# DeltaNet attention and a feed-forward block on one core: a fourth G buffer, key loads from GpSimd's queue, 16-token blocks for chunks 2 and 3, and a new start

## Chip, cores, metric

One core of one Trainium2 chip. The metric is the device time of one launch in microseconds (us). Engines: PE is TensorE, PEld its weight loads, DVE is VectorE, ACT is ScalarE, POOL is GpSimd, SP is SyncE (SPq its queue of transfers).

## The reference, cut to what matters

```python
# q, k, v: (4, 8, 768, 48) fp32; beta: (4, 8, 768)
k_n = k / (norm(k) + 1e-6)
for t in range(768):                      # per batch and head
    y[t]  = q[t] @ state
    v_old = k_n[t] @ state
    state = state + beta[t] * outer(k_n[t], v[t] - v_old)
x  = y as (4, 768, 384)                   # heads side by side
xn = (x - mean) / sqrt(var + 1e-6) * g_ln
out = x + relu(xn @ w_ch1) @ w_ch2        # 384 -> 1536 -> 384; the weights arrive as float64
```

## The kernel before

The 768 tokens are 12 chunks of 64. For a chunk, `p_g` is keys times keys and queries; the triangular matrix made of it is inverted in small diagonal blocks on DVE (lines `tmp` and `xb`), the blocks are put together with matmuls (`p_e`, `p_z`: the join) into `xt`, and then the recurrence runs (`p_by`, `p_u`, `p_s`), which needs the state of the chunk before. Every chunk is followed by its feed-forward (FFN) part, `p_h` and `p_o`, which is the bulk of PE's work. Chunks go in pairs: one inverse serves two. "Boundary" below means the place where a new pair's recurrence starts, seen as the first `p_u` of chunks 2, 4, 6, 8 and 10.

```python
def load_turned(c):                                   # 8 key and 8 query pieces per chunk
    load_blocks(k, c, 0, (nc.sync,))
    load_blocks(q, c, 1, (nc.sync,))
...
def new_chunk(c):
    gsb = work.tile([128, GH, C], FP32, name="gsb", bufs=3)
...
def prep(c):                                          # p_g of a chunk, and what leads to it
    new_chunk(c)
    for n in range(2):
        with tc.issue_after(after) if c < 4 else nullcontext():
            turned(c, n)                              # 32x32 transposes of keys, queries
        yield
    for g in range(2):
        products(c, g, 0, 2)                          # p_g
        yield
    ...
...
with in_this_order(tc) as last:                       # the start is traced in a fixed order
    ...
    joins = [first_join(c) for c in two]              # chunks 0 and 1 joined together
...
plan = Plan()                                         # all else: each step has a planned time
...
for m in range(1, NSL):                               # pairs of chunks
    times = (t - 102, t - 76, t - 38, t - 10) if m > 1 else (4, 22, 58, 74)
    if m > 1:
        for i, c in enumerate(chunks):
            plan.once(times[0] - 20 + 32.5 * i, load_turned, c)
    plan.spread(in_turn(*(prep(c) for c in chunks)), SLAB * N_PREP, times[0], times[1])
    plan.spread(blocks(m, (nc.sync,)), N_BLOCKS + 1, times[1], times[2])   # 32-token blocks
    plan.spread(join(chunks), 5, times[3], t)
plan.run()
```

The plan only fixes the order in which the program is traced. The builder then orders each engine's instructions by its own reckoning of when their inputs will be there; the traces show the engines at work in that built order (in the changed kernel all 848 DVE instructions of the page; of PE's records outside the joins, 6,181 of 6,184).

Of the kernel before, what the change touches and what calls it, by code (L numbers as in the profile page):

```python
# [8 lines left out]
FP32 = mybir.dt.float32  # L9
# [7 lines left out]
C = 64  # L17
DP = 64
BK = 32
FB = 16  # L20
SLAB = 2
# [46 lines left out]
def in_turn(*gens):  # L68
    for gen in gens:
        yield from gen  # L70
# [3 lines left out]
def kernel(  # L74
# [21 lines left out]
    nc = tc.nc  # L96
# [5 lines left out]
    KC = DM // 128  # L102
    FT = DFF // 128
    NP = H // 2
    GH = 2 * H
    TOK = 256

    const = ctx.enter_context(tc.tile_pool(name="const", bufs=1))
    loads = ctx.enter_context(tc.tile_pool(name="loads", bufs=3))
    work = ctx.enter_context(tc.tile_pool(name="work", bufs=2))  # L110
# [29 lines left out]
    def load_blocks(src, c, n, engs):  # L140
        dst = tblocks[(2 * c + n) % NTB]
        for u in range(2):
            toks = slice(c * C + 32 * u, c * C + 32 * u + 32)
            for hp in range(2):
                for m in range(2):
                    w = min(32, D - 32 * m)
                    p0 = DP * hp + 32 * m
                    engs[m % len(engs)].dma_start(  # L148
                        out=dst[p0 : p0 + 32, :, u, 0:w],
                        in_=src[:, hp::2, toks, 32 * m : 32 * m + w].rearrange("b j t d -> t (b j) d"),  # L150
                    )
# [11 lines left out]
    def load_kv(c):  # L163
        load(k_of(c), k, c)
        vs[c] = loads.tile([128, GH, D], FP32, name="v_raw")
        load(vs[c], v, c)

    def load_turned(c):
        load_blocks(k, c, 0, (nc.sync,))
        load_blocks(q, c, 1, (nc.sync,))  # L170

    for i in (0, 2, 1, 3):
        for hp in range(2):
            p0 = DP * hp + 32
# [17 lines left out]
    def fetch_words():  # L192
        if len(words) < len(pieces):
            words.append(early_pool.tile([128, WN, 2], U32, name="words", bufs=3))
            nc.gpsimd.dma_start(
                out=words[-1].rearrange("p n w -> p (n w)"), in_=pieces[len(words) - 1][1]
            )

    for _ in range(2):
        fetch_words()  # L200


    beta_b = const.tile([128, NSL, BK], FP32, name="beta_b")

    beta_f = const.tile([128, 2, FB], FP32, name="beta_f")

    def places():

# [2 lines left out]
                for i in range(2):  # L211
                    yield ((cc * 2 + e) * 2 + i) * GH, cc, e, i

    with nc.allow_non_contiguous_dma(reason="short rows of beta and g_ln"):
        for c in range(2):
            for e in range(2):
                nc.gpsimd.dma_start(
                    out=beta_f[e * C : (e + 1) * C, c],
                    in_=beta[2 * e : 2 * e + 2, :, c * C : (c + 1) * C]
                    .rearrange("g h (b t) -> b (g h) t", t=FB),  # L220
                )
        g_sb = const.tile([128, KC], FP32, name="g_sb")
        nc.gpsimd.dma_start(out=g_sb, in_=g_ln.rearrange("(t p) -> p t", p=128))

    def load_beta():
# [13 lines left out]
    for e in range(2):  # L239
        rows = slice(e * C, (e + 1) * C)  # L240
# [5 lines left out]
    xts = [const.tile([128, GH, C], FP32, name=f"xt{i}") for i in range(NXT)]  # L246
# [4 lines left out]
    states = [const.tile([128, 2, NP, D], FP32, name=f"s{g}") for g in range(2)]  # L251
    for t in states:
        nc.gpsimd.memset(t, 0.0)
    scale_w = const.tile([128, KC + 1], FP32, name="scale_w")
    nc.vector.tensor_scalar_mul(scale_w[:, 0:KC], g_sb, 2.0**-20)
    nc.vector.memset(scale_w[:, KC : KC + 1], 2.0**-20)
    power = const.tile([128, WN], U32, name="power")
    nc.vector.memset(power, 0)
# [34 lines left out]
    def weights(i0, i1, after=None, fetch=True):  # L293
        for i in range(i0, i1):
            with tc.issue_after(after) if after else nullcontext():
                to_fp32(i)
            if fetch:
                fetch_words()
            yield


    made, grams, deep_pools = {}, {}, []
    N_PREP = 4

    def turned(c, n):

        nc.vector.transpose(  # L307
            made[c][0][:, :, n].rearrange("p i (u t) -> p i u t", t=32), tblocks[(2 * c + n) % NTB]
        )
# [35 lines left out]
    def scale_v(c, knrm, eng):  # L345
        eng.tensor_tensor(
            out=vs[c], in0=vs[c], in1=knrm[:, :, None].to_broadcast([128, GH, D]), op=ALU.mult
        )

    def new_chunk(c):  # L350
        gsb = work.tile([128, GH, C], FP32, name="gsb", bufs=3)
        gd = dram.tile([128, GH, C], FP32, name="gd", bufs=2 * SLAB)
        grams[c] = (gsb, gd)
        pool = deep_pools[0] if c % 4 == 0 and deep_pools else work
        made[c] = (pool.tile([128, GH, 2, C], FP32, name="kqt", bufs=1 if pool is not work else 3), [])

    def prep(c):
        new_chunk(c)
        for n in range(2):
            with tc.issue_after(after) if c < 4 else nullcontext():  # L360
                turned(c, n)
            yield
        for g in range(2):
            products(c, g, 0, 2)
            yield
        nc.sync.dma_start(out=grams[c][1], in_=grams[c][0])
# [9 lines left out]
    def prep_g(c):  # L376

        new_chunk(c)
        turned(c, 0)
        for g in range(2):  # L380
            products(c, g, 0, 1)
            yield
        nc.sync.dma_start(out=grams[c][1], in_=grams[c][0])


    N_BLOCKS = 3 + BK // 2
# [17 lines left out]

        return inverse(1, BK, beta_b[:, m : m + 1], gather, scatter)

    def first_blocks(engs):

        def spots():
            for c in range(2):  # L410
                for e in range(2):
                    for b in range(C // FB):
                        p0 = (e * (C // FB) + b) * GH
                        yield p0, c, slice(e * C + b * FB, e * C + (b + 1) * FB), slice(b * FB, (b + 1) * FB)

        def gather(gb):
            for n, (p0, c, rows, cols) in enumerate(spots()):
                engs[n % len(engs)].dma_start(
                    out=gb[p0 : p0 + GH, c], in_=grams[c][1][rows, :, cols].rearrange("s h t -> h s t")
                )  # L420

        def scatter(xd):
            for n, (p0, c, rows, cols) in enumerate(spots()):
                engs[n % len(engs)].dma_start(
                    out=xts[c][rows, :, cols], in_=xd[p0 : p0 + GH, c].rearrange("h s t -> s h t")
                )

        return inverse(2, FB, beta_f, gather, scatter)

    def inverse(nb, L, beta_l, gather, scatter):  # L430

# [244 lines left out]
    two = range(2)  # L676
    with in_this_order(tc) as last:
        for c in two:
            for _ in prep_g(c):
                pass  # L680
        for _ in weights(0, 2, fetch=False):
            pass
        inv = first_blocks((nc.sync, nc.scalar))
        next(inv)
        load_blocks(q, 0, 1, (nc.sync,))
        load_kv(0)
        next(inv)
        for _ in range(3):
            fetch_words()
        for _ in range(FB // 2):  # L690
            next(inv)
        knrm = norms(0)
        turned(0, 1)
        for g in two:
            products(0, g, 1, 2)
        scale_v(0, knrm, nc.vector)
        for _ in inv:
            pass
        load_blocks(q, 1, 1, (nc.sync,))
        load_kv(1)  # L700
        load_turned(2)
        joins = [first_join(c) for c in two]
        next(joins[0])
        turned(1, 1)
        load_turned(3)
        load_beta()
        load_kv(2)
        next(joins[0])
        next(joins[1])
        joined = join(two)  # L710
        next(joined)
        next(joins[1])
        next(joined)
        for g in two:
            products(1, g, 1, 2)
        next(joined)
        next(joined)
        next(joined)
        scale_v(1, norms(1), nc.vector)
    after = last[mybir.EngineType.DVE]  # L720

    T = 45
    starts = [0, 16, 84] + [114 + T * i for i in range(NCH - 2)]
# [1 line left out]
    plan = Plan()  # L725
# [8 lines left out]
    for c in range(NCH):  # L734
        t0, t1 = starts[c], ends[c]
        if c > 1:
            plan.spread(prep_v(c), 2, t0 - 72, t0 - 12)
        plan.once(t0, begin, c)
        plan.spread(in_turn(recur(c, 0), recur(c, 1)), 2 * N_RECUR, t0, t1)
    ffn_0 = ffn(0)  # L740
    plan.spread(ffn_0, FT, 12, 32, whole=False)
    plan.spread(ffn_0, FT, 48, 64)
# [3 lines left out]
    for m in range(1, NSL):  # L746
        chunks = range(SLAB * m, SLAB * m + SLAB)
        t = starts[SLAB * m]
        times = (t - 102, t - 76, t - 38, t - 10) if m > 1 else (4, 22, 58, 74)
        if m > 1:  # L750
            for i, c in enumerate(chunks):
                plan.once(times[0] - 20 + 32.5 * i, load_turned, c)
        plan.spread(in_turn(*(prep(c) for c in chunks)), SLAB * N_PREP, times[0], times[1])
        plan.spread(blocks(m, (nc.sync,)), N_BLOCKS + 1, times[1], times[2])
        plan.spread(join(chunks), 5, times[3], t)
    plan.run()

# [29 lines left out]
```

## Time and profile before

| | before |
|---|---|
| median, range | 714.17 us, 712.36 to 715.97 (4 runs) |
| span, mean granted clock of the profiled run | 712.3 us, 0.923 |
| first `p_u` of chunks 2, 4, 6, 8, 10 | 217.6, 290.0, 390.7, 491.8, 591.2 us |
| longest stretches of PE's built order without an FFN matmul, from chunk 2 on | 326, 235, 236, 236, 222 |

The last row is counted in the built program, not in a trace; the trace shows two matmul records for each of these fp32 instructions (864 of `p_h` for 12 times 36). The page's busy times and the two costliest DVE groups of the kernel before (columns of a group: line, engine, operation, out<-in, shapes, count, busy us, mean ns, idle before it):

```profile
PE 587.3 (82%) x8104; PEld 431.3 (61%) x8104; DVE 363.8 (51%) x874; ACT 152.3 (21%) x410; POOL 77.2 (11%) x130
...
L466 DVE TENSOR_TENSOR xb<-xb,tmp 128x31 f32<-128x31 f32 (+20 forms) x170 | 61.7, 363 | 4.4
...
L461 DVE TENSOR_TENSOR tmp<-xb,gb 128x31 f32<-128x31 f32 (+20 forms) x170 | 57.6, 339 | 5.1
```

PE is the busiest engine, but 18% of the span it has nothing, and part of its busy time runs at half clock (0.50 from 200 to 240 us).

### The profile page before, as it was taken

The page shows a single profiled execution, that of the slowest core. Times are in us where ns is not written, and L with a number is a line of the kernel's source. Part 1 is how long each engine was busy: PE and PEld are TensorE (multiplying, and loading weights), DVE is VectorE, ACT ScalarE, POOL GpSimd, SP SyncE. Part 2 cuts the span into 40 slices and gives each one's busy share as a digit, 9 for nine tenths or more (in the row PEclk, how much of TensorE's full clock was granted, in tenths as well). Part 3 has the DMA queues.
Part 4 walks back from the last instruction along what each step waited for, and adds up shares of the span by engine and source line. Part 5 has one row for each costly group of instructions (what it writes and reads, how often), then busy time and mean ns, then how long its engine had stood idle before and what let it go on. Part 6 is the DMA issues. An engine that isn't in the chain of part 4 may idle for free.

```text
span 712.3 us, 18518 instructions
## 1 busy us (share of the span) xinstructions
PE 587.3 (82%) x8104; PEld 431.3 (61%) x8104; DVE 363.8 (51%) x874; ACT 152.3 (21%) x410; POOL 77.2 (11%) x130
## 2 busy tenths in 40 slices
PE   2035697649956988899988999997999888999997
PEld 2025585327545765785755876755867657868684
DVE  5652889999542397403596412894223973021100
ACT  2011332102022221221212221313222302213120
POOL 7100012111200002000202001102001210010000
PEclk9999999999965799599999699997799995999999
DMA  6865446940345403704505507207215021000000
GB/s 121 176 103 76 86 127 158 197 112 23 73 92 99 64 1 74 116 4 102 81 2 103 89 4 145 37 13 122 58 45 106 1 64 23 0 13 13 12 12 22
DMA packets 210320, 49.29 MB, mean 69 GB/s; under 512 B 204720, under 2 KB 205696, under 8 KB 210240
## 3 DMA queue, kind: packets, MB, share of 16 engines
q1 hardware_dynamic: 197472, 33.81, 26.9%
q0 software_dynamic: 4192, 13.79, 6.7%
q10 hardware_dynamic: 8576, 0.53, 0.8%
q8 instruction: 63, 1.03, 0.6%
q14 instruction: 17, 0.14, 0.1%
HBM read 34.19 MB, written 13.89 MB: 68 GB/s over the span
## 4 chain that ended last, share of the span: by engine, by line
PE 47%; DVE 25%; SPq 9%; DMA 8%; issue 6%; ACT 3%; POOL 2%; DVEq 0%; ACTq 0%; POOLq 0%
PE p_h L646 19%; PE p_o L657 14%; DVE xb L466 7%; DVE tmp L461 7%; SPq L148 5%; PE p_by L571 3%; PE p_g L320 3%; PE p_u L587 2%; DVE kqt L307 2%; SPq L400 2%; DMA k<-in_k_dram 2%; DMA xd<-xb 2%; PE p_by L610 1%; PE p_z L535 1%; PE p_n L633 1%
## 5 line engine op out<-in xcount | busy, mean ns | idle before, releaser
L646 PE MATMUL p_h<-xnt,w_sb 128*128 128x256 f32 x864 | 211.6, 400 | 7.8 <-ACT h_f L651 5.5
L657 PE MATMUL p_o<-w_sb,h_f 128*128 128x384 f32 x576 | 203.9, 496 | 14.2 <-DVE w_sb L288 13.6
L646 PEld LDWEIGHTS p_h<-xnt,w_sb 128*128 128x128 f32 x864 | 167.8, 200 | 37.8 <-ACT h_f L651 7.9
L657 PEld LDWEIGHTS p_o<-w_sb,h_f 128*128 128x128 f32 x576 | 104.3, 190 | 81.0 <-DVE w_sb L288 19.5
L651 ACT ACTIVATE h_f<-p_h 128x256 f32<-128x256 f32 x144 | 55.2, 383 | 173.5 <-PE p_h L646 173.1
L320 PE MATMUL p_g<-kqt 48*64 48x128 f32 (+1 forms) x896 | 35.7, 309 | 43.5 <-DVE kqt L307 37.4
L466 DVE TENSOR_TENSOR xb<-xb,tmp 128x31 f32<-128x31 f32 (+20 forms) x170 | 61.7, 363 | 4.4
L666 POOL DMA_DIRECT2D out_dram<-o x44 | 24.0, 548 | 352.0 <-DVE o L664 270.0
L320 PEld LDWEIGHTS p_g<-kqt 48*64 48x64 f32 x896 | 28.3, 169 | 53.9 <-issue 32.6
L461 DVE TENSOR_TENSOR tmp<-xb,gb 128x31 f32<-128x31 f32 (+20 forms) x170 | 57.6, 339 | 5.1
L327 DVE TENSOR_TENSOR pt<-p_g,pmask 128x512 f32<-128x512 f32 x24 | 16.6, 690 | 74.7 <-ACT gsb L323 70.3
L664 DVE TENSOR_TENSOR o<-p_o,x_ln 128x384 f32<-128x384 f32 x24 | 13.3, 556 | 68.2 <-PE p_o L657 68.2
L571 PEld LDWEIGHTS p_by<-s,kqt 48*64 48x64 f32 x1408 | 30.4, 156 | 14.9 <-issue 9.6
L571 PE MATMUL p_by<-s,kqt 48*64 48x48 f32 x1408 | 35.1, 243 | 3.8 <-ACT x_ln L555 3.8
L540 DVE COPY xt<-p_z 32x256 f32<-32x256 f32 x48 | 20.0, 417 | 33.0 <-PE p_z L535 32.4
L492 PE MATMUL p_e<-xn,gsb 32*32 32x32 f32 x768 | 22.6, 224 | 16.1 <-DVE xn L484 12.7
L307 DVE STREAM_TRANSPOSE kqt<-tb 128x1024 f32<-128x1024 f32 x24 | 29.4, 1235 | 6.9 <-DMA k<-in_k_dram 4.7
L576 DVE TENSOR_TENSOR rhs<-v_raw,p_by 128x384 f32<-128x384 f32 x22 | 12.1, 552 | 37.0 <-PE p_by L571 36.3
L492 PEld LDWEIGHTS p_e<-xn,gsb 32*32 32x32 f32 x768 | 19.8, 137 | 18.6 <-DVE xn L484 12.0
L500 ACT ACTIVATE es<-p_e 32x256 f32<-32x256 f32 x48 | 18.1, 376 | 54.2 <-PE p_e L492 39.4
L535 PE MATMUL p_z<-xt,es 32*32 32x32 f32 x768 | 24.9, 235 | 3.7 <-issue 2.0
L610 PEld LDWEIGHTS p_by<-u,pt 64*64 64x64 f32 x768 | 19.7, 162 | 13.7 <-issue 7.2
(77 smaller groups left out, 468.9 us busy)
## 6 DMA issues: line engine op xcount, KB each, us to landing
words<-in_moe_w_ch_dram POOLq DMA_DIRECT2D x24, 384.0 KB, 3.9
gd<-gsb SPq DMA_DIRECT2D x12, 512.0 KB, 3.0
k<-in_k_dram SPq DMA_DIRECT2D x24, 192.0 KB, 4.1
v_raw<-in_v_dram SPq DMA_DIRECT2D x24, 192.0 KB, 4.4
out_dram<-o POOLq DMA_DIRECT2D x44, 96.0 KB, 2.4
tb<-in_k_dram SPq DMA_DIRECT2D x48, 64.0 KB, 3.0
tb<-in_q_dram SPq DMA_DIRECT2D x48, 64.0 KB, 2.7
gb<-gd SPq DMA_DIRECT2D x40, 64.0 KB, 2.8
```

The source lines that it names most:

```text
L148: engs[m % len(engs)].dma_start(out=dst[p0 : p0 + 32, :, u, 0:w], in_=src[:, hp::2, toks, 32 * m : 32 * m + w].rearrange("b j t d -> t (b ...
L307: nc.vector.transpose(made[c][0][:, :, n].rearrange("p i (u t) -> p i u t", t=32), tblocks[(2 * c + n) % NTB])
L320: nc.tensor.matmul(p_g[toks, hp, j, n0:n1], kqt[rows, i, 0], kqt[rows, i, n0:n1])
L461: nc.vector.tensor_tensor(out=t, in0=xb[:, :, 0:n, j : j + 1].to_broadcast([128, nb, n, w]), in1=gb[:, :, j : j + 1, j + 1 : L].to_broadca ...
L466: nc.vector.tensor_tensor(out=rest, in0=rest, in1=t, op=ALU.subtract)
L492: nc.tensor.matmul(p_e[r1, h % H], gsb[r0, h, BK:C], xn[r0, h])
L535: nc.tensor.matmul(p_z[r0, h], es[r1, h], xt[r1, g * H + h, BK:C])
L571: nc.tensor.matmul(p_by[half(e ^ (hp & n)), hp, n, j], kqt[rows, (2 * e + g) * NP + j, n], s[rows, e, j], start=(n == 0 and j == 0), stop= ...
L610: nc.tensor.matmul(p_by[half(e ^ hp), hp, 1, j], pt[half(e), 2 * j + hp], u[half(e), 2 * j + hp], start=(c == 0 and j == 0), stop=True, sk ...
L646: nc.tensor.matmul(p_h, w1_sb[:, t, f * 128 : (f + 1) * 128], xnt[:, t], start=(t == 0), stop=(t == KC - 1),)
L651: nc.scalar.activation(h_f, p_h, ACTF.Relu)
L657: nc.tensor.matmul(p_o, hs[f][:, g * 128 : (g + 1) * 128], w2_sb[:, f], start=(f == 0), stop=(f == FT - 1),)
```

## The change

Its intent: let the next pair's `p_g` run before the old pair's join has freed a G buffer; get keys in early and off SyncE's queue; make the inverse of chunks 2 and 3 shorter; start chunk 0's recurrence without waiting for chunk 1.

```diff
-    def load_turned(c):
-        load_blocks(k, c, 0, (nc.sync,))
+    def load_turned(c, eng=None):
+        load_blocks(k, c, 0, (eng or nc.sync,))
         load_blocks(q, c, 1, (nc.sync,))
...
-        gsb = work.tile([128, GH, C], FP32, name="gsb", bufs=3)
+        gsb = work.tile([128, GH, C], FP32, name="gsb", bufs=4)
... (prep_p and first_blocks(m) for chunks 2 and 3; beta_f for them)
-        joins = [first_join(c) for c in two]
-        next(joins[0])
+        joining = first_join(0)
+        next(joining)
... (chunk 0's joins alone; chunk 1's become second())
+    plan.spread(second(), 8, 0, 12)
...
-        times = (t - 102, t - 76, t - 38, t - 10) if m > 1 else (4, 22, 58, 74)
+        times = (t - 102, t - 76, t - 38, t - 10) if m > 1 else (1, 7, 30, 74)
         if m > 1:
             for i, c in enumerate(chunks):
-                plan.once(times[0] - 20 + 32.5 * i, load_turned, c)
-        plan.spread(in_turn(*(prep(c) for c in chunks)), SLAB * N_PREP, times[0], times[1])
-        plan.spread(blocks(m, (nc.sync,)), N_BLOCKS + 1, times[1], times[2])
+                plan.once(max(times[0] - 50, 45) + 12 * i, load_turned, c, nc.gpsimd)
+        if m > 1:
+            ... (as before)
+        else:
+            plan.spread(in_turn(*(prep_g(c) for c in chunks)), SLAB * 2, times[0], times[1])
+            plan.spread(in_turn(*(prep_p(c) for c in chunks)), SLAB * 3, 12, 34)
+            plan.spread(first_blocks(m, (nc.sync,)), 3 + FB // 2 + 1, times[1], times[2])
+            plan.spread(in_turn(*(first_join(c) for c in chunks)), 4, 48, times[3])
         plan.spread(join(chunks), 5, times[3], t)
```

More of the change, by code (lines that the diff above doesn't have):

```diff
@@ L197, in fetch_words @@
             )
-    for _ in range(2):
-        fetch_words()
     beta_b = const.tile([128, NSL, BK], FP32, name="beta_b")
-    beta_f = const.tile([128, 2, FB], FP32, name="beta_f")
+    beta_f = const.tile([128, 2 * SLAB, FB], FP32, name="beta_f")
     def places():
@@ L212, in places, with load_beta_f @@
                     yield ((cc * 2 + e) * 2 + i) * GH, cc, e, i
-    with nc.allow_non_contiguous_dma(reason="short rows of beta and g_ln"):
-        for c in range(2):
+    g_sb = const.tile([128, KC], FP32, name="g_sb")
+    def load_beta_f(chunks, eng):
+        for c in chunks:
             for e in range(2):
-                nc.gpsimd.dma_start(
+                eng.dma_start(
                     out=beta_f[e * C : (e + 1) * C, c],
@@ L221 @@
                 )
-        g_sb = const.tile([128, KC], FP32, name="g_sb")
+    with nc.allow_non_contiguous_dma(reason="short rows of g_ln"):
+        load_beta_f(range(2), nc.gpsimd)
         nc.gpsimd.dma_start(out=g_sb, in_=g_ln.rearrange("(t p) -> p t", p=128))
@@ L253 @@
         nc.gpsimd.memset(t, 0.0)
+    for _ in range(2):
+        fetch_words()
     scale_w = const.tile([128, KC + 1], FP32, name="scale_w")
-    nc.vector.tensor_scalar_mul(scale_w[:, 0:KC], g_sb, 2.0**-20)
     nc.vector.memset(scale_w[:, KC : KC + 1], 2.0**-20)
@@ L359, in prep @@
         for n in range(2):
-            with tc.issue_after(after) if c < 4 else nullcontext():
-                turned(c, n)
+            turned(c, n)
             yield
@@ L378, in prep_g @@
         new_chunk(c)
-        turned(c, 0)
+        with tc.issue_after(after) if c >= SLAB else nullcontext():
+            turned(c, 0)
         for g in range(2):
@@ L383, in prep_g, with prep_p @@
         nc.sync.dma_start(out=grams[c][1], in_=grams[c][0])
+    def prep_p(c):
+        turned(c, 1)
+        yield
+        for g in range(2):
+            products(c, g, 1, 2)
+            yield
     N_BLOCKS = 3 + BK // 2
@@ L405, in blocks, with first_blocks @@
         return inverse(1, BK, beta_b[:, m : m + 1], gather, scatter)
-    def first_blocks(engs):
+    def first_blocks(m, engs):
         def spots():
@@ L418, in gather @@
                 engs[n % len(engs)].dma_start(
-                    out=gb[p0 : p0 + GH, c], in_=grams[c][1][rows, :, cols].rearrange("s h t -> h s t")
+                    out=gb[p0 : p0 + GH, c], in_=grams[SLAB * m + c][1][rows, :, cols].rearrange("s h t -> h s t")
                 )
@@ L424, in scatter @@
                 engs[n % len(engs)].dma_start(
-                    out=xts[c][rows, :, cols], in_=xd[p0 : p0 + GH, c].rearrange("h s t -> s h t")
+                    out=xts[SLAB * m + c][rows, :, cols], in_=xd[p0 : p0 + GH, c].rearrange("h s t -> s h t")
                 )
-        return inverse(2, FB, beta_f, gather, scatter)
+        return inverse(2, FB, beta_f[:, SLAB * m : SLAB * m + SLAB], gather, scatter)
     def inverse(nb, L, beta_l, gather, scatter):
@@ L680 @@
                 pass
+        nc.vector.tensor_scalar_mul(scale_w[:, 0:KC], g_sb, 2.0**-20)
         for _ in weights(0, 2, fetch=False):
             pass
-        inv = first_blocks((nc.sync, nc.scalar))
+        inv = first_blocks(0, (nc.sync, nc.scalar))
         next(inv)
@@ L693 @@
         turned(0, 1)
-        for g in two:
-            products(0, g, 1, 2)
-        scale_v(0, knrm, nc.vector)
+        products(0, 0, 1, 2)
         for _ in inv:
@@ L700, with second @@
         load_kv(1)
-        load_turned(2)
-        joins = [first_join(c) for c in two]
-        next(joins[0])
+        load_turned(2, nc.gpsimd)
+        joining = first_join(0)
+        next(joining)
+        products(0, 1, 1, 2)
+        scale_v(0, knrm, nc.vector)
+        next(joining)
         turned(1, 1)
-        load_turned(3)
+        load_turned(3, nc.gpsimd)
+        load_beta_f((2, 3), nc.sync)
         load_beta()
         load_kv(2)
-        next(joins[0])
-        next(joins[1])
-        joined = join(two)
-        next(joined)
-        next(joins[1])
-        next(joined)
+        for _ in join((0,)):
+            pass
+    after = last[mybir.EngineType.DVE]
+    def second():
+        joining = first_join(1)
+        next(joining)
+        yield
+        next(joining)
+        yield
+        yield from join((1,))
         for g in two:
             products(1, g, 1, 2)
-        next(joined)
-        next(joined)
-        next(joined)
+            yield
         scale_v(1, norms(1), nc.vector)
-    after = last[mybir.EngineType.DVE]
+        yield
     T = 45
@@ L748 @@
         t = starts[SLAB * m]
-        times = (t - 102, t - 76, t - 38, t - 10) if m > 1 else (4, 22, 58, 74)
+        times = (t - 102, t - 76, t - 38, t - 10) if m > 1 else (1, 7, 30, 74)
         if m > 1:
             for i, c in enumerate(chunks):
-                plan.once(times[0] - 20 + 32.5 * i, load_turned, c)
-        plan.spread(in_turn(*(prep(c) for c in chunks)), SLAB * N_PREP, times[0], times[1])
-        plan.spread(blocks(m, (nc.sync,)), N_BLOCKS + 1, times[1], times[2])
+                plan.once(max(times[0] - 50, 45) + 12 * i, load_turned, c, nc.gpsimd)
+        if m > 1:
+            plan.spread(in_turn(*(prep(c) for c in chunks)), SLAB * N_PREP, times[0], times[1])
+            plan.spread(blocks(m, (nc.sync,)), N_BLOCKS + 1, times[1], times[2])
+        else:
[3 more added lines that the diff above has]
+            plan.spread(in_turn(*(first_join(c) for c in chunks)), 4, 48, times[3])
         plan.spread(join(chunks), 5, times[3], t)
```

## The prediction

> **What bounds the kernel now.** I read the page first: which slices starve TensorE (PE), and where its granted clock is low. One digit is 17.8 us.
>
> ```profile
> PE   2035697649956988899988999997999888999997
> DVE  5652889999542397403596412894223973021100
> PEclk9999999999965799599999699997799995999999
> ```
>
> PE is short of work up to slice 13 (240 us). Afterwards it has regular dips (slices 16, 21, 27, 33), each with a clock of 5 to 7 beside it. VectorE (DVE) is full in slices 6 to 9. So there are two stages, a start and a PE-bound rest with a dip every 100 us. Next the busy times by window (us, PE, PEld, DVE, ACT, POOL, granted clock, DMA share, GB/s): the weights stage, then chunk 2's stage, then one dip.
>
> ```profile
> 140.00:160.00 20.00, 9.79 (x26) 4.20 (x26) 18.72 (x46) 0.00 (x0) 2.83 (x5) 1.00 0.55 129
> 200.00:220.00 20.00, 10.54 (x294) 8.95 (x295) 8.19 (x14) 3.81 (x10) 0.00 (x0) 0.50 0.35 87
> 220.00:240.00 20.00, 16.09 (x302) 13.46 (x303) 6.06 (x15) 3.82 (x11) 0.00 (x0) 0.50 0.66 102
> 384.00:388.00 4.00, 2.26 (x99) 1.92 (x98) 2.59 (x5) 0.59 (x1) 3.09 (x4) 1.00 0.72 123
> 392.00:396.00 4.00, 3.12 (x118) 2.58 (x115) 1.64 (x4) 1.57 (x5) 0.00 (x0) 0.50 0.65 82
> 404.00:408.00 4.00, 4.00 (x19) 3.51 (x18) 0.62 (x1) 1.15 (x3) 0.00 (x0) 0.95 0.32 51
> ```
>
> From 140 to 160 DVE converts weights and PE waits for it. From 200 to 240 PE runs only joins and chunk 2's recurrence, at half clock. The same happens on a small scale at 384 to 404. Then the timeline there, PE and the SyncE queue, for why.
>
> ```profile
> 383.48 5.18 SPq L400 DMA_DIRECT2D xt<-xd  x8
> 387.98 1.20 PE L492 MATMUL p_e<-xn,gsb 32*32 32x32 f32 x64 [1.60 <-DVE xn L484]
> 390.74 1.55 PE L587 MATMUL p_u<-rhs,xt 64*64 64x48 f32 x32 [0.51 <-DVE xt L540]
> ```
>
> The join (p_e) starts when the inverted blocks (xt) land. The chain of waits leads back from there:
>
> ```profile
> 444.43 3.44 DMA k<-in_k_dram
> 448.24 1.24 POOL xb L455
> 480.35 2.86 DMA xd<-xb
> ```
>
> Keys k land late, because SyncE first issues 16 block loads from 434 to 444. ScalarE's norms wait for them, the inverse's square root stands behind those, and the inverse (449 to 480) with its scatter lands just at the boundary at 490. So the inverse chain sets the 100 us period: chunks 4, 6, 8, 10 first run p_u at 290.4, 391, 492 and 592. In the built instruction order of this kernel every boundary is a block of some 235 matmuls of recurrence and join without one feed-forward (FFN) matmul between them (the trace has two records for each); chunk 2's has 326.
>
> [...] 0.50 from 390 to 404 after the gaps from 384 on, 0.95 by 404 to 408. [...] The trace has 0.42 us for N=256 and 0.19 for N=30, [...] so small inverse steps are mostly fixed cost. [...] SyncE pays 0.49 to 0.53 us per block load. [...] The trace has no 512-piece load from GpSimd, only these two:
>
> ```profile
> 4.11 2.49 POOL L217 DMA_DIRECT2D beta_f<-in_beta_dram  x4
> 6.59 0.81 POOL L223 DMA_DIRECT2D g_sb<-in_moe_g_ln_dram  x1
> ```
>
> 64 pieces each take 0.62, 384 take 0.81. From that I estimate 0.9 to 1.0 us for a key load.
>
> **The change, part by part.**
>
> *16-token blocks for chunks 2 and 3.* Group totals xb 61.7 + tmp 57.6 = 119.3 us are five 32-token inverses and one 16-token one. The 16-token one's 30 steps sum to 7.6 in the timeline, so a 32-token one is (119.3-7.6)/5 = 22.3. Saved 14.7, plus 0.5 on the 128x1024 multiply. Added per chunk: one 1.24 transpose and four half-size copies, two of them on DVE at 0.42; on PE 1.91 for p_e and about 1.0 for p_z. Net DVE -11 us, PE +6 us. In the new order this inverse is finished some 20 DVE instructions before the last weight piece; before, it started there (159.7) and ended at 185.
>
> *Chunk 0 alone.* Before, chunk 0's first p_u ran at 68.95, behind chunk 1's joins. New chain: xn about 41 (xt lands 41.6; g_ln's scale no longer holds chunk 1's transpose, -1.5), p_e 1.9, es 0.4, p_z 1.2 and its gap of 1.6, copies 1.6, q1's transpose 1.25, xn 0.7, two join halves about 4: p_u at 55 to 57. The bulk of the weights may start then, too, instead of at 80.
>
> *Weights stage.* 22 pieces at 2.80 us (start to start, 147.72 to 150.52) are 61.6. The order puts about 39 us of other DVE work among them: 5 transposes 6.3, 6 pt 4.1, chunk 0 and 1's recurrence about 10, chunk 1's join 3, norms and scaling 4, the new inverse 10, rest. That is 101; the same way of counting gives 83 for before's 79, so 97. With 10 us of estimated waits, as chunk 0's round trips are thinly filled: 57+97+10 = 164, against 160. FFN(0) thus ends as before, at about 164, only with the inverse of chunks 2 and 3 done.
>
> *Chunk 2's start.* After that, o and two transposes, then first joins, joins and four p_g between 33 of the 36 p_h of FFN(1). The DVE chain there sums to 17 us; PE has 29. With round trips I take 26 us: p_u of chunk 2 at 190, not 217.6 (-27.6). PE must then do what it did from 217.6 to 290.4 (72.8) plus what is left of FFN(1), 1.3+15.5, less 4 of p_g done, less the half clock and gaps of 217 to 242, about 13: 72 us. Boundary of chunk 4 at 262, not 290.4.
>
> *Fourth G buffer and early keys.* p_g of the next pair moves from +34 us after a boundary to about +13. SyncE has half the loads. Inverse: +13, +10 copies and gather, +2, about 35 interleaved, +7.5 write and scatter, 8 join = 76 us, under the PE work. So the period becomes PE's. The boundary block took 16.0 us (385.28 to 401.26); dense, its work is two p_by at 1.08, p_u and p_by at 0.61, p_n 0.33, four join groups at 1.07 = 8.0. Another 2 us are the half clock until 404.5. I give 1 back for new gaps: 100.4-16+8-2+1 = 91. In the new order 2 to 6 FFN matmuls stand between all steps, about 2.6 us, more than a round trip.
>
> *Sum.* 262 + 3x91 = 535 (592 before). The last stretch takes 120.6 and has one dip, -5.6: 535+115 = 650 us span. The timed median lies 1.5 above the span: **652 us**, -62: about 28 from the start, 28 from three periods, 6 from the end.
>
> **Rivals.** (1) *The inverse still bounds the periods*: 10 us of slack is small, and the GpSimd copy of xb now stands among loads. For it: the old chain bound. Against: two of its delays, late p_g and SyncE's queue, are removed. Then periods stay near 98: 675 to 685. (2) *GpSimd's key loads are slow*: at 3 us or more each, 16 take 48, and weight fetches and transposes wait in line: 690 or more. Against: 0.81 us for 384 pieces. (3) *The weights stage grows*: chunk 1's join among conversions stalls in-order DVE; FFN(0) at 175 gives 663. (4) *Better*: gaps vanish; FFN alone at full clock is 31.0 per chunk, the pair's dense sum about 84, periods 87: 640.
>
> **Range and chances.** Main reading half; (1) in part a quarter; (3) 15%; (2) 10%. Range 636 to 680. Faster by over 2% (below 699.5) fails only if (2) or several meet: 0.93, within 2% 0.05, slower 0.02.
>
> **What would show it.** PE's row without dips at period ends, granted clock 1.0 after about 190, and mean near 0.97, not 0.923. p_u of chunk 0 at 55 to 57, last w_sb near 164, p_u of chunk 2 near 190, chunk 4's 262, periods 91. GpSimd key loads near 1 us. Wrong if: key loads take over 2 us, the last w_sb comes after 172, or p_e at boundaries still waits over 1 us for xn after a scatter, with the clock at 0.50.

The sum comes to 262 + 3x91 + 115 = 650 us of span, 652 as a median. 0.50 and 0.95 are PE's granted clock. N is the number of elements per partition of a two-tensor fp32 step of DVE (`xb`: 0.42 us for 255, 0.20 for 30); by these two, an estimate, some 0.17 us of a step don't depend on N. The issue of one block load on SyncE took a median of 0.49 us in the stretch from 434 to 444. A round trip is a wait such as the printed ones of that boundary, 0.16 to 1.60 us. That the clock would stay up where the order leaves few gaps was the estimate from the windows.

## The result, and the profile after

The changed kernel takes 659.0 us (657.47 to 661.94, 4 runs) against 714.17: ratio 0.9232, 95% interval 0.9192 to 0.9273. Here and below a ratio is the mean time of one kernel's fast runs over that of the other's fast runs of the same rounds, so it is not quite the ratio of the medians. The profiled run has a span of 657.7 us and a mean granted clock of 0.975. The page of the changed kernel, the same lines as before, and the new group of key loads on GpSimd:

```profile
PE 563.2 (86%) x8744; PEld 405.9 (62%) x8744; DVE 350.4 (53%) x848; ACT 155.3 (24%) x416; POOL 128.8 (20%) x210
...
PE   2025878946799899999899999899999999999997
...
PEclk9999999897599899999999999999999999999999
...
L148 POOL DMA_DIRECT2D tb<-in_k_dram x80 | 53.1, 670 | 90.7 <-DVE kqt L309 74.1
...
L476 DVE TENSOR_TENSOR xb<-xb,tmp 128x31 f32<-128x31 f32 (+20 forms) x154 | 53.9, 350 | 3.6
L471 DVE TENSOR_TENSOR tmp<-xb,gb 128x31 f32<-128x31 f32 (+20 forms) x154 | 51.6, 335 | 4.0
```

After slice 13 (230 us) no clock digit is below 9; before, there was one every 100 us. PE has 640 more matmul records than before (320 matmuls) in 24 us less busy time. The windows of the changed kernel around the boundary of chunk 6 (its `p_u` is at 370.93), then PE's timeline there (start, duration, operation):

```profile
366.00:370.00 4.00, 4.00 (x79) 3.33 (x78) 1.25 (x2) 0.94 (x3) 0.63 (x2) 1.00 0.76 196
370.00:374.00 4.00, 4.00 (x48) 3.30 (x47) 0.36 (x1) 1.52 (x5) 0.00 (x0) 1.00 0.50 80
```

```profile
365.57 1.56 PE L656 MATMUL p_h<-xnt,w_sb 128*128 128x256 f32 x6
367.06 1.15 PE L581 MATMUL p_by<-s,kqt 48*64 48x48 f32 x64
368.14 2.86 PE L656 MATMUL p_h<-xnt,w_sb 128*128 128x256 f32 x12
370.93 0.68 PE L597 MATMUL p_u<-rhs,xt 64*64 64x48 f32 x32
```

No idle time is printed in front of any line: while DVE makes `rhs` from `p_by`, PE has six `p_h` to do (twelve records). Before, `p_u` stood right behind the join, in bursts with gaps. Where the 54.6 us between the two spans come from, read off the first `p_u` of each pair:

| stretch | before | after | difference |
|---|---|---|---|
| start to chunk 2 | 217.6 | 199.3 | -18.4 |
| chunk 2 to 4 | 72.4 | 81.6 | +9.2 |
| chunk 4 to 6 | 100.8 | 90.1 | -10.7 |
| chunk 6 to 8 | 101.1 | 91.3 | -9.8 |
| chunk 8 to 10 | 99.4 | 88.4 | -11.1 |
| chunk 10 to the end | 121.1 | 107.1 | -13.9 |

The +9.2 and the -13.9 belong together in part: in the new order nine `p_h` matmuls of the next FFN (some 4.4 us) stand around `p_by` ahead of the `p_u` of a pair, and that work is then missing at the end. Nor is the -18.4 all gain: before the first `p_u` of chunk 2 the old kernel's trace has 96 `p_o` records, the new one's 48. The other 48, some 17 us, now run between chunk 2 and chunk 4, which the prediction had reckoned with. That this stretch grows by only 9.2 us all the same is a large part of the gain: its mean granted clock is 0.96 instead of 0.81.

### The profile page after: what moved, and what is told of

It reads as the page before. It is cut to its first block, busy times and chain, and to the rows that moved or that the text cites. A ratio compares the mean times of both kernels' runs of the same rounds, so it can differ in the third digit from the quotient of the medians.

```text
span 657.7 us, 19778 instructions
## 1 busy us (share of the span) xinstructions
PE 563.2 (86%) x8744; PEld 405.9 (62%) x8744; DVE 350.4 (53%) x848; ACT 155.3 (24%) x416; POOL 128.8 (20%) x210
## 3 DMA queue, kind: packets, MB, share of 16 engines
q8 instruction: 68, 1.11, 0.7%
## 4 chain that ended last, share of the span: by engine, by line
PE 61%; DVE 21%; DMA 6%; issue 5%; SPq 3%; ACT 2%; ACTq 1%; POOL 1%; DVEq 0%; POOLq 0%
PE p_h L656 24%; PE p_o L667 20%; DVE xb L476 5%; DVE tmp L471 5%; PE p_g L322 4%; PE p_by L581 3%; PE p_u L597 2%; PE p_e L502 2%; PE p_z L545 2%; DMA k<-in_k_dram 1%; PE p_s L609 1%; DMA gb<-gd 1%; PE p_n L643 1%; PE p_by L620 1%; SPq L148 1%
## 5 line engine op out<-in xcount | busy, mean ns | idle before, releaser
L667 PE MATMUL p_o<-w_sb,h_f 128*128 128x384 f32 x576 | 208.4, 502 | 14.7 <-DVE w_sb L290 14.7
L656 PEld LDWEIGHTS p_h<-xnt,w_sb 128*128 128x128 f32 x864 | 163.1, 196 | 32.4 <-ACT h_f L661 4.2
L148 POOL DMA_DIRECT2D tb<-in_k_dram x80 | 53.1, 670 | 90.7 <-DVE kqt L309 74.1
L322 PE MATMUL p_g<-kqt 48*64 48x64 f32 (+1 forms) x1024 | 37.1, 293 | 34.9 <-DVE kqt L309 31.4
L476 DVE TENSOR_TENSOR xb<-xb,tmp 128x31 f32<-128x31 f32 (+20 forms) x154 | 53.9, 350 | 3.6
L471 DVE TENSOR_TENSOR tmp<-xb,gb 128x31 f32<-128x31 f32 (+20 forms) x154 | 51.6, 335 | 4.0
L581 PEld LDWEIGHTS p_by<-s,kqt 48*64 48x64 f32 x1408 | 24.6, 140 | 10.7 <-issue 9.6
L564 DVE COPY u<-p_u 64x192 f32<-64x192 f32 x24 | 8.6, 359 | 40.7 <-ACT u L563 40.6
L581 PE MATMUL p_by<-s,kqt 48*64 48x48 f32 x1408 | 27.8, 226 | 0.1
L613 DVE TENSOR_TENSOR s<-s,p_s 128x384 f32<-128x384 f32 x22 | 12.2, 553 | 28.9 <-PE p_s L609 28.6
L502 PEld LDWEIGHTS p_e<-xn,gsb 32*32 32x32 f32 x768 | 16.1, 113 | 12.3 <-issue 11.1
```

The source lines that it names most:

```text
L148: engs[m % len(engs)].dma_start(out=dst[p0 : p0 + 32, :, u, 0:w], in_=src[:, hp::2, toks, 32 * m : 32 * m + w].rearrange("b j t d -> t (b ...
L322: nc.tensor.matmul(p_g[toks, hp, j, n0:n1], kqt[rows, i, 0], kqt[rows, i, n0:n1])
L471: nc.vector.tensor_tensor(out=t, in0=xb[:, :, 0:n, j : j + 1].to_broadcast([128, nb, n, w]), in1=gb[:, :, j : j + 1, j + 1 : L].to_broadca ...
L476: nc.vector.tensor_tensor(out=rest, in0=rest, in1=t, op=ALU.subtract)
L502: nc.tensor.matmul(p_e[r1, h % H], gsb[r0, h, BK:C], xn[r0, h])
L581: nc.tensor.matmul(p_by[half(e ^ (hp & n)), hp, n, j], kqt[rows, (2 * e + g) * NP + j, n], s[rows, e, j], start=(n == 0 and j == 0), stop= ...
```

## The experiments

Two readings had to be told apart first, which the prediction had held together. **Queue**: on the chip, sixteen key and query loads of half a microsecond hold up SyncE's gathers and scatters, so the inverse ends late. **Order**: the chip doesn't mind; but the builder, told that an engine issues the keys, lays out PE's instructions differently, and the layout sets the period. Beside these stood the fourth buffer, the early time of the loads, the blocks and the start. All twelve runs, with the first `p_u` of the pairs in the profiled run:

| run | median us | ratio to before | chunk 2 | 4 | 6 | 8 | 10 |
|---|---|---|---|---|---|---|---|
| before | 713 to 714 | 1 | 217.6 | 290.0 | 390.7 | 491.8 | 591.2 |
| changed kernel | 659.0 | 0.9232 | 199.3 | 280.8 | 370.9 | 462.2 | 550.6 |
| e1 three G buffers | 656.3 | 0.9217 | 195.9 | 277.5 | 367.6 | 458.7 | 547.4 |
| e2 keys on SyncE | 711.4 | 0.9968 | 226.6 | 297.2 | 396.9 | 498.6 | 602.4 |
| e3 keys late | 656.3 | 0.9203 | 201.4 | 278.3 | 369.2 | 460.1 | 548.4 |
| e4 32-token blocks | 672.5 | 0.9442 | 197.4 | 277.4 | 383.9 | 474.8 | 563.5 |
| e5 joins together | 664.2 | 0.9319 | 208.8 | 287.1 | 378.3 | 469.5 | 557.9 |
| e6 before, 4 buffers | 712.7 | 0.9992 | 218.4 | 291.0 | 391.6 | 491.4 | 591.3 |
| e7 before, 4 buffers, keys | 670.0 | 0.9387 | 201.2 | 281.6 | 385.4 | 476.6 | 564.9 |
| e8 fillers | 657.5 | 0.9212 | 196.8 | 279.3 | 368.9 | 459.7 | 548.0 |
| e9 SyncE, good order | 665.0 | 0.9330 | 203.5 | 282.2 | 372.6 | 464.1 | 552.4 |
| e10 GpSimd, bad order | 710.6 | 0.9957 | 228.1 | 297.7 | 397.6 | 497.6 | 602.9 |
| e11 before, keys only | 667.7 | 0.9351 | 203.2 | 275.6 | 380.2 | 471.5 | 559.9 |
| e12 p_h inside the join | 658.2 | 0.9233 | 201.1 | 280.8 | 370.9 | 462.0 | 550.4 |

All give the right result.

**e1: the changed kernel with three G buffers.**

```diff
-        gsb = work.tile([128, GH, C], FP32, name="gsb", bufs=4)
+        gsb = work.tile([128, GH, C], FP32, name="gsb", bufs=3)
```

> The changed kernel with three G buffers instead of four; its instruction order is the same. Main theory T (the periods shortened because the instruction order puts feed-forward matmuls between the boundary's steps, and the inverse ends early enough because keys no longer queue behind SyncE's loads): the fourth buffer matters little, 659 to 668 us, periods (p_u of chunk 4 to 6 to 8 to 10) 90 to 92. Rival A (the fourth G buffer is what lets the next pair's p_g run early): the p_g copies wait for the old buffer until the boundary's join, and PE, in order, waits behind them: periods 97 to 100, 680 to 690 us.

Measured 656.3 us, ratio 0.9217 (0.9185 to 0.9249): the same as with four. The built order is the same too.

**e6: the kernel before with four G buffers** (the same line, the other way).

> The kernel before with four G buffers and nothing else; the instruction order is that of before. Theory T: 708 to 714 us, periods 99 to 101, as the keys still land late. Rival A (fourth buffer is the lever of the periods): periods 92 to 95, 690 to 697 us.

Ratio 0.9992 (0.9964 to 1.002). The fourth buffer does nothing in either kernel. Rival A is out.

**e2: the changed kernel, keys issued by SyncE.**

```diff
-                plan.once(max(times[0] - 50, 45) + 12 * i, load_turned, c, nc.gpsimd)
+                plan.once(max(times[0] - 50, 45) + 12 * i, load_turned, c)
```

(and the same for chunks 2 and 3 in the start)

> The changed kernel with all key block loads issued by SyncE again, at the same planned times. Theory T (SyncE's queue held the inverse chain): gathers and scatters of the inverse stand behind 16 loads of 0.5 us again, and the built order has boundary blocks of 128 to 231 matmuls without feed-forward work: periods back at 97 to 100 and 680 to 692 us. Rival A (fourth buffer): periods stay near 91, 659 to 665 us. Rival B (it is the early time of the loads, not the queue, that counts): also 659 to 665.

711.4 us, ratio 0.9968 (0.9947 to 0.9989). The whole gain but 0.3% is gone, more than expected: the periods are back at 99.8, 101.6 and 103.9 us, and chunk 2 starts later than in the kernel before. So fourth buffer, early time, small blocks and the new start together are worth 0.3% as long as SyncE issues the keys and the builder orders the rest.

**e7: the kernel before with four G buffers and the early keys on GpSimd.**

```diff
-                plan.once(times[0] - 20 + 32.5 * i, load_turned, c)
+                plan.once(max(times[0] - 50, 45) + 12 * i, load_turned, c, nc.gpsimd)
```

(and the same for chunks 2 and 3 in the start, and `bufs=4`)

> The kernel before with four G buffers and with the key loads on GpSimd's queue at the early times; the start is that of before. Theory T: the built order then has only one long block without feed-forward work after chunk 2's, the periods become 91 (three of them and the last stretch gain, about 34 us), chunk 4's p_u stays at 288 to 290: 678 to 684 us. If the starts and the periods are worth the same whatever the other does, before minus this one and this one minus the changed kernel add up to 55. Rival (the short periods need the new start as well): 695 us or more.

670.0 us, ratio 0.9387, better than expected. The old start and the old blocks reach chunk 2 at 201.2, about as early as the changed kernel (199.3). The parts don't add up: these two, 6.1%, and all the rest, 0.3% by e2, make 6.4%, while together they are worth 7.7%.

**e11: the kernel before with one line changed.**

```diff
-        load_blocks(k, c, 0, (nc.sync,))
+        load_blocks(k, c, 0, (nc.gpsimd if c > 1 else nc.sync,))
```

> The kernel before with one line changed: key blocks from chunk 2 on are issued by GpSimd, at the old late times, with three G buffers, old start, old block sizes. Its built order is nearly that of the run that also had the fourth buffer and early times (670.0 us). If neither buffer nor time matters: 668 to 673 us, periods of 91 from chunk 6 on. If one of them is needed: 680 us or more.

667.7 us, ratio 0.9351 (0.9330 to 0.9372), with the old three buffers, late times, old start and old blocks. This one line is 6.5 of the 7.7%.

**e3: the changed kernel with the loads at the old late times**, still on GpSimd.

```diff
-                plan.once(max(times[0] - 50, 45) + 12 * i, load_turned, c, nc.gpsimd)
+                plan.once(times[0] - 20 + 32.5 * i, load_turned, c, nc.gpsimd)
```

> The changed kernel with the key and query loads at the late times of the kernel before, keys still issued by GpSimd. The built instruction order is that of the changed kernel. Theory T (queue, not time): SyncE's share is halved and the inverse chain has some 10 us to spare, so 659 to 668 us, periods 90 to 93. Rival B (the early time counts): keys land up to 20 us later, norms and the square root of the inverse wait, periods 95 to 100, 675 to 690 us.

656.3 us, ratio 0.9203 (0.9174 to 0.9231). The early time is worth nothing; the built order is nearly that of the changed kernel (rebuilt, PE's differs in 12 of 4413 places and DVE's in 112 of 853). Rival B is out. What is left is the issuing engine, through the queue or through the order.

**e9: keys on SyncE as in e2, but with the order of the changed kernel.** The order of PE, DVE and ACT was read from the changed kernel's built program and pinned; only the queues of transfers are left to the builder.

```diff
     plan.run()
+    force_order(tc)     # for PE, DVE, ACT: each instruction depends, for its place only,
+                        # on the one ahead of it in a recorded list
```

> The key loads issued by SyncE as in the run with the keys on SyncE (711.4 us), but with the instructions of TensorE, VectorE and ScalarE pinned to the very order that the changed kernel has (656 to 659 us). It parts the two ways in which the issuing engine can act. Theory O (the gain is the built order: with slow SyncE issues the builder expects keys late and puts the next chunks' work into one lump at the boundary): 656 to 672 us, periods 90 to 95. Theory Q (the gain is the queue on the chip: the loads hold up gathers and scatters whatever the order): 690 to 712 us, periods 97 to 104, PE waiting at the boundaries.

**e10: the reverse, keys on GpSimd with the order of e2**, by the same means.

> The reverse: the changed kernel with its key loads on GpSimd, but the three engines pinned to the order of the kernel with the keys on SyncE. Theory O: the bad order costs what it cost there, 695 to 712 us, with boundaries of 127 to 231 matmuls without feed-forward work and a half clock behind them. Theory Q: keys and scatters come early, PE finds its data ready in any order and only the round trips remain: 656 to 680 us.

e9 takes 665.0 us, ratio 0.9330 (0.9304 to 0.9357); e10 takes 710.6 us, ratio 0.9957 (0.9934 to 0.998). With the good order SyncE may issue all the keys; with the bad order GpSimd's help is worth nothing. The order carries the gain. Pinning as such costs nothing that can be seen: e10 has the order of e2 and its time, 710.6 against 711.4. The orders of PE, DVE and ACT were moved together, so these two runs don't say which engine's order counts; what follows about that is read from the windows. The windows of e10 around its boundary of chunk 6 (`p_u` at 397.56), PE's timeline there with the idle time in front of a step in brackets, and the scatter in SyncE's queue with the step of DVE that needs it:

```profile
388.00:392.00 4.00, 4.00 (x57) 2.49 (x51) 1.25 (x2) 0.59 (x1) 0.00 (x0) 1.00 0.46 57
392.00:396.00 4.00, 2.40 (x140) 2.17 (x132) 1.77 (x3) 1.04 (x3) 1.09 (x2) 1.00 0.64 176
396.00:400.00 4.00, 2.68 (x66) 2.09 (x66) 1.31 (x4) 1.46 (x5) 0.00 (x0) 0.66 0.46 71
400.00:404.00 4.00, 3.72 (x112) 3.33 (x112) 1.14 (x3) 0.87 (x3) 0.00 (x0) 0.50 0.77 102
404.00:408.00 4.00, 3.97 (x118) 3.32 (x113) 2.28 (x5) 2.35 (x7) 0.00 (x0) 0.50 0.06 8
```

```profile
388.41 2.85 PE L748 MATMUL p_o<-w_sb,h_f 128*128 128x384 f32 x8
391.18 1.10 PE L403 MATMUL p_g<-kqt 48*64 48x128 f32 x32
392.11 1.10 PE L662 MATMUL p_by<-s,kqt 48*64 48x48 f32 x64
394.80 1.20 PE L583 MATMUL p_e<-xn,gsb 32*32 32x32 f32 x64 [1.59 <-DVE xn L575]
396.36 0.69 PE L626 MATMUL p_z<-xt,es 32*32 32x32 f32 x32 [0.36 <-ACT es L591]
397.56 1.55 PE L678 MATMUL p_u<-rhs,xt 64*64 64x48 f32 x32 [0.51 <-DVE xt L631]
```

```profile
378.27 5.12 SPq L491 DMA_DIRECT2D xt<-xd  x8
...
394.04 0.70 DVE L575 STREAM_TRANSPOSE xn<-xt 128x512 f32<-128x512 f32 x1
```

The last piece of `xt` is issued by 383.4, and such pieces take a median of 2.6 us to land: it is there at about 386. The order holds it up on two engines. PE is still on FFN matmuls, which stand ahead in its order, and comes to `p_by` only at 392.11; on DVE `xn` stands behind `rhs`, which waits for `p_by`, so it starts at 394.04 and `p_e` at 394.80. Behind that the order has no FFN left, so each small step pays its round trip (0.36, 0.51, 0.43 and 0.29 us printed); the clock falls to 0.50, and it stays there for some 13 us (0.66 and 0.64 in the windows at its two ends). These traces give no rule for the fall: here it comes within 396 to 400, and the gaps printed up to there are 1.59, 0.36 and 0.51 us, 2.5 together; in the changed kernel PE is busy for only 1.31 of the 4 us from 64 to 68, with a gap of 2.69 us, and the clock stays at 1.00. The cost of this one boundary, an estimate that counts busy time below full clock as lost in proportion (in the kernel before, 10 `p_h` records fill the 4 us from 236 to 240 at 0.50, 21 those from 408 to 412 at 1.00; small ones differ less, 32 `p_z` records here 1.06 us at 407.52 and 0.69 at 396.36), from these windows and the next, 408 to 412 (4.00 busy at a mean clock of 0.64): idle 1.60 + 1.32 + 0.28 = 3.2 us; time lost to the clock 2.68 x 0.34 + 3.72 x 0.50 + 3.97 x 0.50 + 4.00 x 0.36 = 6.2 us; 9.4 in all. The period of e10 is 99.8 there and that of the changed kernel 90.1. e9 at its own boundary (`p_u` at 372.63), with SyncE's key loads of this stretch:

```profile
368.00:372.00 4.00, 4.00 (x78) 3.33 (x77) 1.25 (x2) 0.77 (x2) 0.34 (x1) 1.00 0.84 204
372.00:376.00 4.00, 4.00 (x48) 3.02 (x46) 0.36 (x1) 1.40 (x4) 0.00 (x0) 1.00 0.45 72
```

```profile
311.09 5.03 SPq L214 DMA_DIRECT2D tb<-in_k_dram  x8
...
353.51 3.31 SPq L214 DMA_DIRECT2D tb<-in_k_dram  x4
```

Full and at full clock, although SyncE spends 5 us on eight key loads. Its periods are 90.4, 91.4 and 88.4 us, those of the changed kernel to 0.4 us. What the queue costs is about the 1% between 0.9330 and 0.9232 (0.3 to 1.7% with the two intervals). The profiled run of e9 is the fastest of its four and shows only 1.8 us of it in its span: the last weight piece is ready at 165.4 instead of 159.6 and chunk 2 comes 4.3 us later, of which 1.4 are left at chunk 4.

The next pair's inverse, too, starts late through the order. The second G of the next pair leaves for memory 24 us after the boundary in e10 (321.98, boundary at 297.73), and 10 us after it both in e9 (292.00, 282.19) and in the changed kernel (290.64, 280.83), since `p_g` stands there in PE's order.

**e4: the changed kernel with 32-token blocks for chunks 2 and 3.**

```diff
-            plan.spread(first_blocks(m, (nc.sync,)), 3 + FB // 2 + 1, times[1], times[2])
-            plan.spread(in_turn(*(first_join(c) for c in chunks)), 4, 48, times[3])
+            plan.spread(blocks(m, (nc.sync,)), N_BLOCKS + 1, times[1], times[2])
```

> The changed kernel with chunks 2 and 3 inverted in one 32-token block each as before, and no first joins for them. Theory T: the inverse takes 15 us more of VectorE between the weight conversions and after them, so it ends after the last weight piece, chunk 2's p_u comes at 210 to 216 instead of 199, and 670 to 678 us in all; periods stay near 90. Rival (the longer inverse fits beside the weights stage's waits, the 32-token form costs PE less): 655 to 662 us.

672.5 us, as expected in size, but in another place. Chunk 2 isn't late at all (197.4). The loss is one boundary further on, 106.5 us from chunk 4 to 6 instead of 90.1; in e4's windows ahead of and behind chunk 4's `p_u` at 277.44, and PE's longest wait there:

```profile
265.00:280.00 15.00, 8.08 (x230) 6.46 (x228) 5.70 (x15) 2.62 (x7) 2.02 (x3) 0.80 0.65 142
280.00:300.00 20.00, 19.81 (x299) 16.32 (x303) 4.13 (x9) 5.27 (x14) 0.00 (x0) 0.72 0.10 19
```

```profile
273.94 1.92 PE L502 MATMUL p_e<-xn,gsb 32*32 32x32 f32 x64 [4.72 <-DVE xn L494]
```

Chunk 4's inverse comes 16 us later here (its blocks are written at 266.48, against 250.74 in the changed kernel), and the built order has one stretch of 227 matmuls without FFN at this boundary. Which of the two costs the time, no run parts. e7 and e11, with 32-token blocks too, show the same long interval (103.8 and 104.6 us).

**e5: chunks 0 and 1 joined together, as before.**

```diff
+        joins = [first_join(c) for c in two]
... (the start of the kernel before; second() is gone)
-    plan.spread(second(), 8, 0, 12)
```

> The changed kernel with chunks 0 and 1 joined together before the weights and the recurrence start, as before. Theory T: chunk 0's p_u at 67 to 70 instead of 61, the bulk of weight conversions starts later by as much, last w_sb at 164 to 170 instead of 159.6, chunk 2's p_u 5 to 9 us later, 664 to 670 us. Rival (the weights stage is bound by VectorE's sum of work, which is the same either way, and by the arrival of words): the last w_sb within 2 us of 159.6 and 658 to 661 us.

664.2 us, ratio 0.9319 (0.9291 to 0.9347), against 0.9232: 0.9%, some 6 us. Chunk 0's `p_u` is at 71.5 instead of 61.0, the last weight piece is ready at 176.7, later than expected, and chunk 2 comes 9.5 us later; a part comes back later on.

**e8: filler matmuls in the weights stage.** Chunk 2 starts 9 us later than predicted, and in the changed kernel the clock is at 0.50 just there (and from 156 to 160; from 160 to 164 it is 0.96):

```profile
164.00:168.00 4.00, 2.40 (x195) 1.97 (x198) 0.20 (x1) 0.88 (x2) 3.88 (x7) 0.89 0.70 155
168.00:172.00 4.00, 1.17 (x92) 1.02 (x80) 0.69 (x1) 0.25 (x2) 1.03 (x2) 0.50 0.20 38
172.00:176.00 4.00, 4.00 (x50) 2.66 (x53) 3.67 (x5) 0.95 (x3) 0.00 (x0) 0.50 0.02 4
```

```profile
166.68 0.30 PE L527 MATMUL p_e<-xn,gsb 32*32 32x16 f32 x13 [1.28 <-issue]
...
171.42 0.35 PE L534 MATMUL p_z<-xt,es 32*16 32x16 f32 x22 [2.83 <-issue]
```

```diff
+    def keep_warm(first, n):
+        for f in range(first, FT):
+            p_w = ps_att([128, DM], "p_w")
+            for _ in range(n):
+                nc.tensor.matmul(p_w, ident, w2_sb[:, f])
+            yield
+    plan.spread(keep_warm(2, 2), FT - 2, 32, 52)
```

> The changed kernel with 20 filler matmuls of 128 by 384, two behind each of the last ten weight pieces, so that PE is not idle for long between 120 and 160 us. It tells what the half clock at 156 to 182 costs. If the miss of 10 us at chunk 2's start is the half clock: granted clock 1.0 at 160 to 182, chunk 2's p_u at 189 to 193, 650 to 655 us. If it is waits between the small steps (round trips), p_u stays at 197 to 200 and the time at 657 to 662 although the clock is up. If the fillers only delay VectorE or PE: over 662.

657.5 us, ratio 0.9212 (0.9175 to 0.925), chunk 2 at 196.8. The clock is up until about 171 (0.90 from 168 to 172), but a gap of 1.6 us inside `p_z` is still there, and the clock falls after it all the same (0.50 from 172 to 176). Of the 9 us the fillers bring 2.5 at most, which is within the scatter of runs that have the changed kernel's order or nearly so (195.9 in e1, 201.4 in e3).

**e12: FFN matmuls inside chunk 2's first join.** PE and DVE pinned to the changed kernel's own order, but five groups of `p_h` put between the small matmuls:

```diff
     plan.run()
+    force_order(tc)    # p_g, p_e 16, p_h, p_e 16, p_h, p_e 32, p_h, p_g, p_z 32, p_h, p_z 32, ...
```

> The changed kernel with TensorE and VectorE pinned to its own order, except in the stretch of 303 TensorE instructions between the last weight piece and chunk 2's joins: there the five groups of three feed-forward p_h matmuls that stood behind and between chunk 2's first join are put inside it, one after each 16 or 32 of its small matmuls. It tells what the 10 us are by which chunk 2's start was later than predicted. If they come from the gaps of 1.3 and 2.8 us inside the dense runs of small matmuls and from the half clock (0.50) that follows them from 168 to 181 us: no gaps over 1 us there, clock 0.9 or more, chunk 2's p_u at 190 to 194 and 648 to 653 us. If the stage is long for its sum of work and its round trips alone: p_u at 196 to 200 and 656 to 660 us.

658.2 us, ratio 0.9233 (0.9198 to 0.9267), chunk 2 at 201.1: nothing gained. The gaps inside that join are gone, but others stand around it, in PE's timeline of e12:

```profile
163.01 0.89 PE L380 MATMUL p_g<-kqt 48*64 48x128 f32 x24 [1.21 <-issue]
...
194.31 0.48 PE L380 MATMUL p_g<-kqt 48*64 48x128 f32 x4 [1.73 <-issue]
```

A gap that ends at "issue" is one in which PE waits for nothing that the profile's waits show. The transfers in the kept traces point to PE's own instructions. The page lists a queue of 16 KB "instruction" packets. Its bytes go with the number of PE records: 1.03 MB for 16,208 in the kernel before, 1.11 MB for 17,488 in the changed one (matmuls and weight loads). In the changed kernel two of these packets ended at 165.26 and 169.89, and the two gaps of it printed under e8 at 166.68 and 171.42, so 1.4 and 1.5 us later. Of e12's two, the one that ends at 194.31 ended 1.2 us after such a packet; the one at 163.01 did not follow one. Of the 72 gaps at "issue" of over 0.8 us in the traces of all runs (after the first 30 us), 66 ended 1.2 to 1.9 us after such a packet (9 of 10 in the kernel before and the changed one). No run tests it, but it fits that the gaps come where many small matmuls follow each other, as in the first joins of the 16-token blocks.

## Why the prediction was right in time and wrong in cause

- **The total.** 652 predicted, 659.0 measured, inside the range. That it fell so close is partly luck, for it is a sum of errors that cancel in part: chunk 2 +9.3 us, chunk 2 to 4 +9.6, three periods -3.3, the last stretch -7.9; together +7.7.
- **"So the inverse chain sets the 100 us period", with keys late behind SyncE's loads.** This step failed. The chain of waits was read rightly, but it was a chain through an order: in e10 the keys come from GpSimd and the period stays at 100 us; in e9 they come from SyncE and it is 90. What set the period was the built order. That it is the lump of some 235 matmuls of join and recurrence in it, with `p_g` of the next pair late, is read from the windows of e10; the runs show it only for the order as a whole.
- **"In the new order 2 to 6 FFN matmuls stand between all steps."** This step held at the later boundaries (at chunk 4's one stretch of 80 matmuls without FFN is left), and the short periods rest on it. It was found in the built order, and the sum for the period rests on it (16.0 us of boundary to 8, and the half clock): 91 predicted; 90.1, 91.3 and 88.4 measured. The period came out right because it was worked out from the lump, not from the chain.
- **"Fourth G buffer and early keys."** Nothing: e1, e6 and e3. That `p_g` moved to +10 us after the boundary is the order again, with three buffers as well.
- **"SyncE has half the loads."** True and worth about 1% (e9).
- **16-token blocks.** DVE's two groups fell from 119.3 to 105.5 us, 13.8 against 14.7 predicted. Their worth is right in size (e4: 0.9442 against 0.9232, some 15 us) but not in place: not chunk 2's start, but chunk 4's boundary, where the inverse is no longer late.
- **Chunk 0 alone.** `p_u` at 61.0, predicted 55 to 57; last weight piece at 159.6, predicted 164; worth 6 us (e5).
- **"With round trips I take 26 us", for the stage from the end of FFN(0) to chunk 2.** This term was mis-sized: the last `p_o` of FFN(0) ends at 161.5 and `p_u` starts at 199.3, so it took 38 us. The text itself had 29 us of PE work there, so 26 could not hold. To the 29 come 4.4 us idle between 164 and 172 and about 5 for the half clock (2.40 x 0.11 + 1.17 x 0.50 + 8.00 x 0.50 + 4.00 x 0.10 = 5.2 in the windows from 164 to 184). Neither e8 nor e12 moved chunk 2's start by more than the scatter; a remedy was not found.
- **Chunk 4's boundary at 262.** It came at 280.8: 9.3 us are chunk 2's. Of the other 9.6, some 4.4 are the moved FFN work, which the last stretch gives back; some 5.5 are a stall at 220 to 232 us, where `p_n` waits 2.75 us for `xn_ln` (ahead of it one `xb` step of DVE took 2.15 us, its neighbours 0.3 to 0.4) and the clock falls behind it (2.08 us busy at 0.65 and 4.00 at 0.50, so 2.7 us more). The text had no such stall.
- **Rivals.** (1) did not come; its argument, a tight inverse, is what e4 shows at one boundary. (2): a key load takes 0.67 us on GpSimd (mean of the 64 KB and the 32 KB ones), not 3, and those of 64 KB a median of 3.4 us from issue to landing; the estimate of 0.9 to 1.0 was too high. (3): the weights stage did not grow. (4) came in part: the boundaries have hardly a gap left.
- **Readings.** The clock did fall at about 390 (0.84 from 388 to 392, then 0.50); the longest idle time printed at that boundary is 1.60 us. The two small loads are not all that GpSimd issued before: its page has 24 loads of `words` and 44 stores as well, at 0.55 us each. And the first `p_u` of chunks 4 and 10 are at 290.0 and 591.2, not 290.4 and 592.

That a different issuing engine makes the builder choose a different order is shown: e2 and the changed kernel differ in nothing else, and their built orders have stretches of up to 231 and of up to 80 matmuls without FFN behind chunk 2's first join (which is itself in a stretch of 144 in the changed kernel). Why it chooses so, presumably because it reckons SyncE's loads as slow, is argued and not shown (on the chip a block load's issue took a median of 0.49 us on SyncE in the kernel before, and 0.65 on GpSimd in the changed one).

No run beats the changed kernel by more than its spread: e1, e3 and e8 lie within 0.3% of it. The simplest kernel as fast as it is the one with three buffers or late loads.

## What to carry to other kernels

When a builder orders the instructions, a change to a load may act through the order alone. Compare the built orders first, and before believing a cause on the chip, pin the order and move the load, then move the order and leave the load: two runs parted here what the trace alone had not. And look for the longest stretch of the bound engine's order without filler work: the one lump of small dependent steps that is reckoned up here (e10) cost some 9 us, a third of it as idle time and two thirds as half clock behind it.
